# Attention with chunk selection and a wave mixer: batch 1's later keys copied once from PSUM, three blocks of u turned by DMA, and a new instruction order

## The chip, the cores and the metric

The kernel runs on one core of a Trainium2 chip. The metric is the device time of one launch in microseconds. A core has five engines that each run their own instruction stream in order: TensorE (PE in the profile, with its weight loads as PEld), VectorE (DVE), ScalarE (ACT), GpSimd (POOL) and SyncE (SP), which here issues all DMAs.

## The reference

The reference is selective attention followed by a mixer. Sizes: 4 batches, 8 heads, 768 positions, head size 64; the mixer's width is 512.

```python
k_chunks = k.reshape(B, H, nc, chunk, D)           # 24 chunks of 32 keys
k_min, k_max = k_chunks.min(axis=3), k_chunks.max(axis=3)
ub = sum(maximum(q * k_min, q * k_max), axis=-1)   # bound of each query for each chunk
top_chunks = argsort(where(causal, ub, -1e9))[..., -6:]
scores = where(selected & causal, q @ k.T / 8, -1e9)
x = softmax(scores) @ v                            # heads side by side: 4 x 768 x 512

theta = x @ w_theta
y = w_tok_r @ (x * cos(theta)) + w_tok_i @ (x * sin(theta))
u = x + y
out = u + maximum(u @ w_ch, 0)
```

## The kernel before, in words

The kernel records some 1,400 small operations in `record` and emits them in the order of the string `ORDER`. Each number there is an operation; a letter behind it picks another of the engines that the operation may run on ("b" the second, "c" the third of its list; no letter is the first). F with a number is a run of filler matmuls on PE. Every engine executes its share in the order of the string, so `ORDER` alone decides both who does what and when. Buffers are handed out by `decode` as the string is walked: each class in `CLASSES` has a fixed number of slots, and an operation that needs a slot waits for the last user of its former tenant. Loads have 6 slots ("ld"), PSUM has two wide score tiles ("sc"), one "av" bank and three general banks ("mi").

Attention works on pairs of heads, four pairs in a batch. For a pair of batches 1 to 3, `pair` (L417) loads keys and queries with 128 positions to a partition row, and turns them on PE with the help of an identity (L434), 384 positions to a PSUM bank. It does this:

- Keys. For each half of the positions, four instructions read the bank: two copies of one head each into the fp16 key tile `kx` (the `evk` operations), and a maximum and a minimum over each chunk (`red0`, `red1`, L451), which give the chunk bounds `km`.
- Queries. One fp32 copy per half into `qT` (`evq`), two fp16 casts from it into `qx` (`cq`), and a relu of it (`relu`, on DVE or POOL at L195, on ACT at L197).
- Bounds and selection. `group` (L474) multiplies bounds and queries of two pairs (`ub`, L491), turns the result on DVE, takes the sixth largest value of each query, and copies a mask into rows 64 to 88 of `qx` (`cp`, L536). `kx` has the matching one-hot rows, so a score product adds the penalty by itself.

`heads` (L543) forms scores in three steps per head (`sc`, L564), takes the exponential on ACT (`ex`, L570), zeroes the later triangle (`tri`, POOL at L580 or DVE at L578), and multiplies with v (`av`, L402); DVE divides by the sum (`norm`, L412 and L413). Batch 0 does the same with other tiles (`row_pair`, `row_heads`).

`mixer` (L587) then turns x (on PE for batches 0 and 1, by DMA from SP for 2 and 3, L600), multiplies by w_theta (`th`, L617), takes sin and cos on ACT (L624, L628), forms `z`, and for each of six blocks of 128 rows multiplies by the token weights (`mix`, L640 and L642: twelve matmuls of 512 columns). DVE adds x (`u`, L648). Each block of u is turned, and multiplied by w_ch (`ch`, L673); DVE forms the output (`ot`, L678) and SP stores it. How a block is turned hangs on a set:

```python
if (b, t) in U_DMA:
    op("SP", f"Du.{b}.{t}", 1270, [(u[t], 0)], [(uT[t], 0)], ...)   # one DMA transpose
    continue
ps = buf("mi", f"ups.{b}.{t}", (DM,), FP16)                         # else PE and a copy
op("PE", f"Tu.{b}.{t}", 220, [(u[t], 0)], [(ps, 0)], tr)
ev16(f"evu.{b}.{t}", ps, uT[t], DM)
```

The weights are loaded during batch 0, cast to fp16 by POOL, ACT or DVE, and turned by DMA (token weights of four row blocks) or by PE (of two). In the string, attention of batch b+1 is woven into the mixer of batch b.

The set `K_SB` is in the code already, and empty. A pair in it copies its turned keys to a tile `kT` and works from there:

```python
kT = buf("qT", f"kT.{b}.{p}") if (b, p) in K_SB else None
...
for x in range(2) if kT is not None else ():
    copies(f"ck.{b}.{p}.{x}", S, 0, False, [(kT, 0), (kT, 1)], [(kx, (x, 0)), (kx, (x, 1))], ...)
```

Of the kernel before, what the change touches and what calls it, by code (L numbers as in the profile page):

```python
# [15 lines left out]

ORDER = (
    "10|"
    "3 2 448 4 449b 404b 1 722b 475b 29 28 31 30 0 21 57 17 58 9 18 5 721 19b 14 7 15 56 6 F9 32 20c 10 36 55 "
    "11 35 39 48 12 F17 44 34 13b 8 41 33 85 23 45 75 16c 42 37 47b 38 22 24 84 40 25 F15 50 102 26 68 27 403 "  # L20
    "71 51 69 180 82 52 72 174 181 83 63 175 74 165 65 182 59 64 166 171 49 373 60 374 61 172 168 176b 53 115 "
    "169 67 54 F7 177 173 167b 77 62b 43 46b 170b 178 76c 95 78 125 66 206 179 191 79 96 189 207 103 188 192 "
    "200 80 183 113 208b 201 187 81 193 194 190 184 195 202 90 197 91 203 196 92 198 98 70c 86 73c 141 204 185 "
    "116 88 223 109 199 87 144 99 217 205 186 224 215 126 213 214 211 89 114 209 216 400 226 218 225 399 269 "
    "94 129 101 227 210 127 270 142 220 212 128b 104 133 110c 221 143 228b 219b 145 271 93 105 229 376 272b "
    "106 222 384 137 230 379 375 107 232 402 387 410 100 233 401 108 236 381 97 377 414 386 231 258 412b 380 "
    "234 255 146 385b 130 259 235 237 256 388 246 260 238 239 134 247 240 249 383 257 411b 241 111 250 252 153 "
    "248b 382 253 242 243 251 131 389b 474 378 413 244 273 254 263 132 267 138c 274b 135 245 262 159 266 136b "
    "265 139 268 261 390 140b 264 392 391 418 150 393 275 419 112 416 276 396b 405 394 123 277 417 408 117 "
    "422b 395 407b 162 281 409 278 154 406b 289 415b 147 160 425 155 290 420c 279 285 421c 282 161 280 283 426 "  # L30
    "124 286 435 156 297 427b 287 151 428 119 291 293 284 152 118b 315 288 299 316 429 121 298 317 292 397 295 "
    "301 430 163 302 294 436 437 318 148b 432c 446 308 434c 447 309 296 444 310 445 300 311 319 438 320 431 "
    "149 433 303 157 321 515 439 544 516 120c 304 158 122c 305 440c 347 306 443c 423 348 312 441c 307 468 313 "
    "545 517 471 528 314 343 442b 361 546 470 344b 529 557 164 362 461 463 558 462b 530 554 464b 455 398b 472 "
    "450 559 457b 560 363 465 322 451 459 473 323 452 458 324 467b 466c 494 325 453 456 326 561 454 327 424c "
    "741 345 555 534 328 460b 355 562 535 469 346 349 720 356 518 556 565 350 358 519 357 536b 481 719 359 520 "
    "476 483 563 479 547 482 717 336 477b 548 337 484 745 338 478 549 485 339 746 480 340 341 486b 718 487 342 "
    "489 488 531 495 490 364 743 532 492c 491 353 365 521 493b 541 789 533 522 564 496 742 566 354b 366 542 "
    "523 744 370 497 506 543 786 524 498 526 371 507b 734 736 787 508 329 737 330 735b 372 331 509 739b 332 "
    "499 738 788 333 740b 510 334 765 500 760 511c 335 525 761 360 728 512c 527 351 513c 730 758 352 586 729 "  # L40
    "514c 808 550 501 759 552 551 731 504c 367 587 732 764c 553 723 747 725 810 368 583 748 811 538 727 588 "
    "539 584 369 763 537 750 752 751 606 753 1053 502c 726 580 749 1054 585 755 607 733b 803 540 505c 503c 754 "
    "724b 609 608 804 756 619 762 581 621 620 790 757b 622b 766 591 793 570 792b 610 809 767 813 791b 812 582 "
    "571 794 1056 612 611 768 589 1055 590 613 777 572 573 795 592 769b 574 614 814 832 599 778b 796b 615 575 "
    "617 600 779 567 616 797 601 770 596 568 780 771 597 578 781 569 593 772 784c 576 785b 577 799 598 594 892 "
    "798 774c 618 819 800b 815 776c 898 1079 823 893 801 595 1080 579 775c 1078 899 895 894 816b 1077 802 603 "
    "900 818 885 896 807c 602 817 604 827 820b 623 886 605 882 828 879 897 624 883 903 887 625 822 805 902 880 "
    "626 1057 901 1061 884 631 821 806 904 627 633 1060 881 773 889 1058b 890 888 1059b 853 856 629 891 635 "
    "632 782 783 628 643 634 636 630 637 639 824 644 833c 647 645 638 1075 640 679 646 641 680 681 648 642 651 "
    "649 652 857 653 650 654 682 1076c 683 1120 684 1121 854 825 858 685 869 1099 655 826 855b 697 866 870 831 "  # L50
    "656 829 834 867 657 830 693 1068 835 872 868 1069 844 859 871 672 873 836 845b 837 673 1100b 874 674 846 "
    "658 860 1142 659 838 847 660 839 861 661 848 841b 699 840 851b 849 842 843b 662 852c 700 663 850c 877 701 "
    "875 664 908 918 694 909 1062 1086 1063b 876 919 910 947 1144 1090 675 1145 1089 1064 920 676 878 1087 677 "
    "1088 950 1065 864 862 1066 711 678 702 1067 712 696 1070 703 1094 1071 863 713 1095b 665 704 1073 948 865 "
    "1123 666 1081 1122 1072c 951 1092 1146 934 1084 949 1143b 1147 911 1093b 667 1166 1074 1082 668 1098b "
    "1096c 669 1085 1097 670 912 708 671 1083 1091b 935 924 952b 695 709 1101 925 913b 936b 1137 710 1102 926 "
    "905 1111 1103b 921 1138b 906 1112b 686 1104 1124 922 1135 907 1128 916 944 1105 1136 914 923b 931 1106 "
    "945 1139 915 1125b 705 1141b 917 1140 937 932 1127 687 1108c 706 927 1109c 929 1107b 688 1113 933 707 "
    "1110b 689 946 938 928 1114 1219 930 1167 1126 953 955 1213 1220 1115 939 1129 1214 954 1221 1132 1216 "
    "1117c 1133 941 1119c 1217 942 1131b 690 1215 691 956 1118c 1130 940 1218 1193 692 1226 1134b 1194 1116c "  # L60
    "1161 943 698 1148 1227 1195 1229 1162b 1222 1151 1223 1230 957 1228 1224 1149b 1232 1159 1225 1233 1153 "
    "1231 958 1206 1150 1157 1187 1234 1207 1160b 1236 1237 1156 959 1235 1188 1165c 714 1238 1154 1200 1152 "
    "961 1155 1190 715 1158b 1201 963 1189 1208 960 1191 1168 1163c 1164c 965 962 1202 1203 1169 1192 1198 "
    "1178 971 1170 1179b 716 1171 1196 964 1197 1180 967 972 973 1172 975 966 968 974 969 983 1199 976 979 977 "
    "970 985 1001 978 1002 981 1173 1003 980 1181 1004 1177 984 982 1022 1204 1023 986 1005 1182 994 1176 995 "
    "1184 996 1186 1183 1185b 1006 1174 1175b 1205 1255 1007 1258 1256 1209 1211 1031 1008 1009 1259 1257b "
    "1252 1260 1210 1253 1278 1212 997 1279 1010 1254b 1263 1239 1262 1280 1240 1261 1245 1264 998 1246 1024 "
    "1241b 1271 1025 1247 1272 1265 1026 1273b 1266 1242 1011 1243 1012 1267 1284 1027 1285 1244 1250 1281 "
    "1028 1286 1248 1249 1282 1034 1041 1251 1283 1268 1042 1013 1269 999 1043 1014 1288 1287 1270 1000 1276 "
    "1032 1289 1015 1290 1274 1275 1016 1030 1277 1017 1018 1019 1291 1020 1050 1021 1292 1044 1051 1293 1038 "  # L70
    "1045 987 1039 1294 1297 988 1299 1295 1301 989 1296 990 1298 991 1302 992 1300 1040 1305 1303 1033 993 "
    "1304b 1309 1306 1052 1307 1313 1046 1310 1029 1317 1311 1308 1314 1342 1312 1315 1343 1344 1319 1316 1345 "
    "1318 1335 1320 1336 1337 1338 1339 1340 1346 1341 1347 1328 1365 1348 1329 1330 1331 1366 1321 1322 1323 "
    "1324 1325 1326 1047 1327 1332 1048 1363 1333 1356 1334 1357 1049 1358 1359 1377 1380 1378 1364 1360 1381 "
    "1361 1379 1349 1382 1362 1350 1035 1351 1036 1352 1374 1037 1353 1375 1354 1369 1376 1355 1371 1370b 1367 "
    "1372 1389 1368b 1373 1386 1390 1383 1387 1391 1384 1388 1385 "
)

B, H, S, D = 4, 8, 768, 64
P = 128  # L80
DM = H * D
NT = S // P
CH = 32
NCH = S // CH
QS = 192
NS = S - QS
RUN = NS // 2
NB = RUN // CH
SCALE = float(1.0 / np.sqrt(D))
NEG = -1000.0  # L90
KX = D + NCH
ROW = (0,)
X_DMA = (2, 3)
K_SB = set()
LAST = (3, 4)
W_DMA = (2, 3, 4, 5)
U_DMA = {(b, t) for b in (1, 2, 3) for t in range(NT) if b < 3 or t < 4}
SEGS = [(0, 4), (1, 3), (2, 5)]
BASE = [0, 1024, 2048]

# [58 lines left out]
def record(G):  # L159
# [257 lines left out]
    def pair(b, p):  # L417
# [18 lines left out]

        kT = buf("qT", f"kT.{b}.{p}") if (b, p) in K_SB else None
        for f in range(2):
# [481 lines left out]
```

The softmax here doesn't subtract the row's maximum and nothing guards it: scores larger than these inputs give would overflow.

## Time and profile before

| | us |
|---|---|
| median of 4 runs (lowest to highest) | 227.96 (227.54 to 229.69) |
| the profiled execution, its own time | 227.6 |
| its span, first to last instruction | 225.9 |
| PE busy | 215.9 (96%) |
| DVE busy | 173.5 (77%) |
| ACT busy | 164.9 (73%) |
| POOL busy | 93.3 (41%) |
| 16 DMA engines, the hardware queue's share | 70.0% |

A row of a group gives the line, engine, operation, names and shapes, then the total busy time, the mean of one in ns, and the idle time of the engine just before these instructions with what ended it. Rows of stages give each engine's busy time in a stretch of the span, counted in us from its start. The granted PE clock is 1.00 all through.

### The profile page before, as it was taken

Reading aid. Unit: us, or ns where it says so; the run is one execution under the profiler, and the core shown is the slowest. Engines: PE = TensorE matmul, PEld = TensorE weight load, DVE = VectorE, ACT = ScalarE, POOL = GpSimd, SP = SyncE. Lnnn points to the kernel's source line nnn. Section 1 sums busy time; section 2 is a strip of 40 time slices with the busy share of each in tenths; the row PEclk is TensorE's granted clock in tenths of the full one; section 3 lists DMA queues with packets and bytes.
Section 4 is the critical chain, followed back from the end, with each engine's and each line's share of the span. In section 5 each row is a group of like instructions: output and inputs, shape, how many; then the busy total and the mean of one; then the engine's idle time right before and its main releaser. Section 6 shows DMA issues by size and latency. Waiting matters only on the chain.

```text
span 225.9 us, 5663 instructions
## 1 busy us (share of the span) xinstructions
PE 215.9 (96%) x2122; PEld 127.2 (56%) x2122; DVE 173.5 (77%) x505; ACT 164.9 (73%) x247; POOL 93.3 (41%) x190
## 2 busy tenths in 40 slices
PE   7999999989999999888999999999989999999993
PEld 2765766834566667566545665677445564444441
DVE  4699789699889699899977899999885366242553
ACT  2759999999498758999998559899998870560011
POOL 8524647554424648869306223586401130300000
PEclk9999999999999999999999999999999999999999
DMA  6999899999999999976038469413511025562254
GB/s 162 272 263 233 274 312 279 244 304 208 288 251 211 280 254 279 235 179 139 4 70 186 120 115 262 115 48 68 101 47 23 3 70 101 88 186 46 79 178 164
DMA packets 103471, 38.07 MB, mean 169 GB/s; under 512 B 97436, under 2 KB 97820, under 8 KB 103444
## 3 DMA queue, kind: packets, MB, share of 16 engines
q1 hardware_dynamic: 103444, 37.71, 70.0%
q8 instruction: 17, 0.28, 0.5%
q14 instruction: 10, 0.08, 0.1%
HBM read 26.17 MB, written 6.29 MB: 144 GB/s over the span
## 4 chain that ended last, share of the span: by engine, by line
PE 73%; ACT 13%; DVE 4%; DMA 3%; SPq 3%; issue 1%; DVEq 0%; ACTq 0%
PE y L640 13%; PE y L642 13%; PE sc L564 9%; PE ch L673 8%; PE av L402 7%; PE th L617 6%; ACT pt L358 4%; ACT pt L570 3%; PE qps L434 2%; PE kps L434 2%; PE ub L491 2%; PE ub L278 2%; SPq L600 2%; ACT kx L169 2%; DMA xT<-x 2%; PE sc L342 2%
## 5 line engine op out<-in xcount | busy, mean ns | idle before, releaser
L570 ACT ACTIVATE pt<-sc 128x1024 f16<-128x1024 f32 (+1 forms) x72 | 63.3, 919 | 8.8 <-PE sc L564 8.1
L640 PE MATMUL y<-z,wtokT 128*128 128x512 f16 x144 | 54.6, 379 | 0.1
L642 PE MATMUL y<-z,wtokT 128*128 128x512 f16 x144 | 54.5, 379 | 0.0
L580 POOL TENSOR_SCALAR_AFFINE_SELECT pt<-pt 128x256 f16<-128x256 f16 x62 | 25.5, 416 | 49.1 <-ACT pt L570 47.7
L564 PE MATMUL sc<-qx,kx 88*128 88x512 f16 (+3 forms) x192 | 37.2, 305 | 1.2 <-ACT pt L570 1.0
L402 PE MATMUL av<-v,pt 128*128 128x65 f16 x672 | 30.6, 194 | 0.9 <-ACT pt L570 0.8
L402 PEld LDWEIGHTS <-pt 128*128 128x128 f16 x672 | 27.6, 98 | 6.9 <-ACT pt L570 1.4
L648 DVE TENSOR_TENSOR u<-y,x 128x512 f16<-128x512 f32 x24 | 16.4, 689 | 14.3 <-PE y L642 14.1
L451 DVE TENSOR_REDUCE km<-kps 128x12 f32<-128x384 f32 x48 | 25.1, 545 | 1.5 <-PE kps L434 1.1
L617 PE MATMUL th<-wtheta,xT 128*128 128x512 f16 x96 | 22.7, 379 | 1.6 <-DVE ubT L507 0.9
L564 PEld LDWEIGHTS <-kx 88*128 88x128 f16 x192 | 16.6, 97 | 13.2 <-issue 2.6
L673 PE MATMUL ch<-wch,uT 128*128 128x512 f16 (+1 forms) x96 | 23.6, 374 | 0.0
L642 PEld LDWEIGHTS <-wtokT 128*128 128x128 f16 x144 | 14.0, 98 | 15.1 <-issue 0.9
L640 PEld LDWEIGHTS <-wtokT 128*128 128x128 f16 x144 | 14.0, 97 | 15.1
L678 DVE SCALAR_TENSOR_TENSOR ot<-ch,u 128x512 f32<-128x512 f32 (+1 forms) x24 | 16.3, 678 | 7.5 <-PE ch L673 7.3
L632 DVE TENSOR_TENSOR z<-x,cs 128x1024 f16<-128x1024 f16 x23 | 17.0, 759 | 5.8 <-ACT cs L628 3.5
L628 ACT ACTIVATE cs<-th,pi 128x512 f16<-128x512 f32 x24 | 16.2, 697 | 6.8 <-PE th L617 6.3
L169 ACT COPY qT<-qps 128x384 f32<-128x384 f32 x24 | 11.2, 485 | 13.6 <-PE qps L434 6.9
L358 ACT ACTIVATE pt<-sc 128x1024 f16<-128x1024 f32 (+1 forms) x24 | 20.9, 928 | 0.3 <-PE sc L350 0.2
L172 POOL CAST qx<-qT 64x768 f16<-64x768 f32 (+1 forms) x18 | 14.5, 812 | 10.6 <-ACT qT L169 6.5
L413 DVE TENSOR_TENSOR x<-av,rec 128x384 f16<-128x384 f32 x32 | 17.8, 557 | 1.1
L169 ACT CAST kx<-kps 64x384 f16<-64x384 f32 (+1 forms) x36 | 16.8, 478 | 2.3 <-PE kps L434 1.0
(103 smaller groups left out, 339.0 us busy)
## 6 DMA issues: line engine op xcount, KB each, us to landing
q<-in_q_dram SPq DMA_DIRECT2D x32, 192.0 KB, 3.7
k<-in_k_dram SPq DMA_DIRECT2D x32, 192.0 KB, 3.7
v<-in_v_dram SPq DMA_DIRECT2D x16, 384.0 KB, 4.1
out_dram<-ot SPq DMA_DIRECT2D x23, 256.0 KB, 2.3
wtok<-in_moe_w_tok_r_dram SPq DMA_DIRECT2D x6, 384.0 KB, 4.4
wtok<-in_moe_w_tok_i_dram SPq DMA_DIRECT2D x6, 384.0 KB, 5.5
wth<-in_moe_w_theta_dram SPq DMA_DIRECT2D x4, 256.0 KB, 4.2
wch<-in_moe_w_ch_dram SPq DMA_DIRECT2D x4, 256.0 KB, 5.5
```

The source lines that it names most:

```text
L169: c = {"A": ("ACT", int(n * 0.833 + 60), 0, lambda: nc.scalar.copy(out=out(), in_=in_())), "D": ("DVE", int(n / 0.96 + 70) if psum else in ...
L358: nc.scalar.activation(out=T(pt)[:, :, base:base + w], in_=T(ps).rearrange("p (x c) -> p x c", x=2)[:, :, 0:w], func=AF.Exp, bias=0.0, sca ...
L402: nc.tensor.matmul(ps[:, t, :], T(pt)[:, x, o:o + P], T(v16)[:, x, j, :], start=(j == 0), stop=(j == t))
L413: nc.vector.tensor_tensor(out=T(x16)[:, :, h * D:(h + 1) * D], in0=ps[:, :, 0:D], in1=T(rec).broadcast_to([P, NT, D]), op=ALU.mult)
L451: nc.vector.tensor_reduce(out=T(km)[:, j, 12 * f:12 * f + 12], in_=src.rearrange("p (c w) -> p c w", w=CH), axis=AX.X, op=o)
L564: nc.tensor.matmul(T(ps)[:, a0:a1], T(kx)[0:KX, x, j * P:(j + 1) * P], T(qx)[0:KX, x, q0 + a0 - o:q0 + a1 - o], start=True, stop=True)
L570: nc.scalar.activation(out=T(pt)[:, x, BASE[s]:BASE[s] + w], in_=T(ps)[:, 0:w], func=AF.Exp, bias=0.0, scale=SCALE)
L580: eng.affine_select(out=a, in_=a, pattern=[[0, 2], [1, P]], compare_op=ALU.is_ge, fill=G.zero_reg(), base=0, channel_multiplier=-1)
L617: nc.tensor.matmul(T(ps), T(xT[t])[:, c, :] if by_dma else T(xT[c])[:, t * P:(t + 1) * P], K.wtheta[:, c, :], start=(c == 0), stop=(c == 3))
L640: nc.tensor.matmul(T(ps), K.wtok[:, si, 0, t * P:(t + 1) * P], T(z[si])[:, 0], start=(si == 0), stop=False)
L642: nc.tensor.matmul(T(ps), K.wtok[:, si, 1, t * P:(t + 1) * P], T(z[si])[:, 1], start=False, stop=(si == NT - 1))
L673: nc.tensor.matmul(T(ps)[:, 0:n1 - n0], T(uT[t])[:, c * P:(c + 1) * P], K.wch[:, c, n0:n1], start=(c == 0), stop=(c == 3))
```

## The change

Three constants change; no line of a function does.

- `K_SB` holds pairs 2 and 3 of batch 1. Their turned keys leave each PSUM bank in one fp32 copy of 128 x 384 to `kT` (a slot of the class "qT"); the chunk maxima and minima read `kT`, and two casts of 64 x 768 per pair make the fp16 keys.
- `U_DMA` holds blocks 3, 4 and 5 of batch 0 too. Each is turned by one DMA transpose from SP in place of four matmuls and a copy out of PSUM.
- `ORDER` is another string. Apart from the operations above, 112 operations run on another engine than before, and nearly all stand in another place. There are 43 filler matmuls in it where there were 48.

```diff
-    "3 2 448 4 449b 404b 1 722b 475b 29 28 31 30 0 21 57 17 58 9 18 5 721 19b 14 7 15 56 6 F9 32 20c 10 36 55 "
...
+    "2 3 0 1 401b 29 28 4 30 31 400 21 58 5 57 9 12 56 F7 32 8 36 55 6 719 14 35 7 472 17 39 48 11 446 15 18 "
...
-K_SB = set()
+K_SB = {(1, 2), (1, 3)}
 LAST = (3, 4)
 W_DMA = (2, 3, 4, 5)
-U_DMA = {(b, t) for b in (1, 2, 3) for t in range(NT) if b < 3 or t < 4}
+U_DMA = {(b, t) for b in range(4) for t in range(NT) if (b < 3 or t < 4) and (b, t) not in ((0, 0), (0, 1), (0, 2))}
```

Counted over the two strings, the moves between engines are these (operations before, then after):

| | ACT | DVE | POOL |
|---|---|---|---|
| key copies out of PSUM (`evk`) | 36, 32 | 20, 20 | - |
| key casts (`ck`) | 0, 2 | 0, 1 | 0, 1 |
| query copies (`evq`) | 24, 23 | 8, 9 | - |
| query casts (`cq`) | 3, 5 | 11, 9 | 18, 18 |
| relus | 8, 6 | 4, 3 | 4, 7 |
| mask copies (`cp`) | 9, 14 | 14, 9 | 25, 25 |
| triangles (`tri`) | - | 17, 6 | 79, 90 |
| weight casts | 2, 7 | 4, 4 | 14, 9 |
| v casts (`cv`) | 3, 5 | 4, 3 | 9, 8 |
| turned u (`evu`) | 4, 2 | 4, 3 | - |

The order of SP's loads and of its DMA transposes changes with the string as well: at the start the keys of the first pair come first, and the three new transposes stand among the loads of batch 2.

## Prediction

> **What bounds the kernel now.** I read the page's first two parts first, then single matmuls in the timeline, then busy times by stage, then the chain of waits inside the one stage that stood out, and last the groups with their shapes kept apart.
>
> ```profile
> PE 215.9 (96%) x2122; PEld 127.2 (56%) x2122; DVE 173.5 (77%) x505; ACT 164.9 (73%) x247; POOL 93.3 (41%) x190
> ...
> PEclk9999999999999999999999999999999999999999
> DMA  6999899999999999976038469413511025562254
> ```
>
> TensorE (PE) looks full, at full clock throughout, and the DMA engines are full until slice 17 (about 96 us). But the next view shows how little "busy" means for PE.
>
> ```profile
> 150.88 0.38 PE L640 MATMUL y<-z,wtokT 128*128 128x512 f16 x1
> 151.10 0.38 PE L642 MATMUL y<-z,wtokT 128*128 128x512 f16 x1
> 151.31 0.38 PE L640 MATMUL y<-z,wtokT 128*128 128x512 f16 x1
> ```
>
> Each row lasts 0.38 us, yet the next starts 0.22 us later. The page's 96% would leave 10 us of PE outside its work. The Trainium skill (Perfetto Trace Analysis, "Identifying the Most-Contended Engine") calls matmul busy share a poor measure because matmuls overlap; so I count the distance between starts, taken where nothing waits: mixing pair 0.43, head's score step 0.43/0.43/0.27, block of th or ch 0.86, three turns 0.33, one ub 1.13 (1.33 in batch 0). Over all of PE's instructions that gives 205 us. The span is 225.9, so some 21 us are start, end and stalls, and a new order can move those. Where they sit, by stage (us of each engine in each stretch):
>
> ```profile
> 46.00:54.00 8.00, 7.05 (x58) 2.73 (x56) 7.72 (x21) 7.45 (x13) 3.70 (x7) 1.00 1.13 222
> 54.00:86.00 32.00, 32.00 (x273) 19.23 (x272) 27.38 (x82) 23.47 (x37) 15.17 (x30) 1.00 1.14 266
> 86.00:104.00 18.00, 15.62 (x214) 10.78 (x211) 16.96 (x56) 16.89 (x26) 14.20 (x32) 1.00 0.87 206
> 104.00:120.00 16.00, 16.00 (x148) 9.56 (x145) 13.66 (x30) 15.91 (x25) 5.52 (x9) 1.00 0.34 77
> ```
>
> The columns are length, PE, weight loads, DVE, ACT, POOL, clock, DMA share, GB/s. From 54 to 86 PE never rests, while ACT is idle for 8.5 us. From 86 to 104 ACT and DVE are nearly full and PE loses 2.4 us of busy time. The chain of waits there runs through ACT:
>
> ```profile
> 87.57 0.48 ACT kx L169
> ...
> 88.54 0.92 ACT pt L570
> ...
> 97.39 0.70 ACT pt L570
> ...
> 98.62 1.94 ACT pt L570 x2
> ```
>
> These are key evictions of batch 2 and exponentials of batch 1. So two regimes follow each other: PE-bound, then ACT-bound. From 104 us the PE stalls are small.
>
> **The change, part by part.** Prices come from these rows:
>
> ```profile
> L169 ACT CAST kx<-kps 64x384 f16<-64x384 f32 x29 | 13.6, 473 | 1.6 <-PE kps L434 1.0 <-DVE km L451 0.2
> L171 DVE CAST kx<-kps 64x384 f16<-64x384 f32 x19 | 10.4, 547 | 1.1 <-PE kps L434 0.9
> L195 POOL TENSOR_SCALAR qr<-qT 128x576 f32<-128x576 f32 x4 | 6.6, 1646 | 1.9 <-ACT qT L169 1.2 <-DVE qT L171 0.6
> L593 ACT COPY uT<-ups 128x512 f16<-128x512 f16 x4 | 2.3, 587 | 19.9 <-PE ups L661 19.9
> ```
>
> and, of the turned u (issue times of SP, then issue to landing):
>
> ```profile
> L654 SPq DMA_TRANSPOSE uT<-u x16: 1189/1200/2047, 119.7 to 213.1; - x16
> ...
> DMA to landing us min/median/max: 2.4/2.5/4.0
> ```
>
> *Keys of two pairs.* Eight half-width copies out of PSUM go (six of 0.47 on ACT, two of 0.55 on DVE: 3.9 us); four full-width copies come, three on ACT (0.485 by the row of qT) and one on DVE (0.55), 2.0 us; four casts from SBUF come, two on ACT (0.83), one on DVE (0.56 by the median of that cast of queries), one on POOL (0.87), 3.1 us. Sum: +1.2 us, spread over three engines. In return a PSUM bank has one reader instead of four, about 1.5 us less hold for each of four banks. The group of key turns has 0.0 us of idle before it, so I value it at nothing; if the bank is the bound, it gains up to 1.5 us once. The reductions (0.545 from PSUM) now read SBUF, which no row shows; I take the same price, with 0.4 and 0.6 as ends, 8 x 0.1 on DVE. A rule speaks against the casts: the Trainium skill (SBUF — State Buffer, "Who interferes with whom") says a DVE copy or cast that runs in its two-port mode locks POOL out for its whole length, while a reduction doesn't. The row for the same cast of queries on DVE has median 0.56 and longest 1.17 us. By the rule POOL loses the whole 0.5 to 1.2 us once; by the row the DVE cast costs 0.56 and POOL has 5 us of idle time in each 10 there. I take nothing, and 1.2 us as the upper end.
>
> *Turned u of three blocks.* PE loses 3 turns of 4 x 0.055: -0.66 us. One eviction leaves ACT (0.59), two leave DVE (0.41 each). Three DMAs of 1.2 us issue join SP's queue, +3.6 us. They stand behind Lv.1.3, Lk.2.1.1 and Lq.2.2.1, and the loads of batch 2 stand behind them. Before, those loads land 2 to 7 us ahead of their turns; I take 0, with 1.5 as upper end. Then the wait: between the last mixing product of the block and its ch the new order has 9.8 us of PE work for block 3, 9.9 for block 5, 6.9 for block 4. The way round is 0.9 (u on DVE with latency), 0.5 of SP, and 2.5 to 4.0 landing; with DMA full I take 4.0: 5.4 us. All three are covered, block 4 by 1.5 us; if DVE or SP is more than that late, ch of block 4 and all PE behind it wait.
>
> *New order.* It moves most. Over the whole program, with the distances between starts, ACT goes from 144.3 to 149.9 us, DVE from 158.8 to 154.9, POOL from 80.6 to 84.5; the sin/exp table changes stay 8. DVE sheds 11 triangle masks and 5 nsT copies; ACT takes weight copies and five nsT copies; POOL takes the masks and goes from 4 to 7 relus at 1.65 us (ACT 0.69, DVE 0.45).
>
> Until batch 0's mixing the two orders cost the same. From the first exponential to the first sin/cos ACT has 30.3 us in both, and the first mixing product waits for the same cos of block 3 (33.9 then, 33.4 now). At the start the ninth load gates the last q turn in both. One new wait: DVE casts wch.3 ahead of the first z; it was 4.9 us from issue to use before, on POOL. Behind it queue cq, z and the two ub transposes that free PSUM for th of blocks 5 and 4. I put +0.4 against the -0.4 of the mixing's start.
>
> The stage that decides is first mixing product to last exponential of batch 1, before 53.84 to 101.04 = 47.2 us. Sums inside it:
> - PE 44.0 before, so stalls are 3.2; now 42.5 (three turns less; the rest of the difference is work ordered to other places).
> - ACT 34.1 before with one table load, traced 37.6 busy (ratio 1.10); now 39.0, so 43.0. It has 3 more weight copies, 1 more of v, 2 cq, 2 qT, 2 nsT and the 2 key casts (7.1 us); 3 key copies, a relu and a turned-u eviction fewer (2.2 us).
> - DVE 38.7 before, traced 41.9 (1.08); now 35.3, so 38.2.
>
> So the exponentials are spread: by the end of block 5's mixing ACT has 20.1 us of work where it had 14.2, beside 21.3 of PE where it had 20.5. The ACT idle time of 54 to 86 gets used, but by added work as much as by old work. Now every helper must be read against PE: before, PE 44.0 with the fullest helper (DVE) at 41.9 lost 3.2; now PE 42.5 has ACT at 43.0. I let the stall grow by the same 1.1 us: 4.3. Bounds: ACT needs 43.0 - 42.5 = 0.5 at least; if ACT keeps 6.5 of the 9.6 us (47.2 - 37.6) idle, 7.0.
>
> After that: PE and ACT work up to the end are equal within 0.5 us, and DVE has 2.8 us less queued ahead of th of batch 2 (PE 1.0 less), where th of block 3 waited 0.9 us for its turned x. But th of block 0 now needs the second turned x instead of the first (+1.26 of SP). I take -0.3 (+1 to -0.9). Out and end are alike.
>
> Sum against the profiled execution (227.6; span 225.9 and 1.7 around it): -0.66 + 1.1 - 0.3 = +0.1, so 227.7. The median of the runs shown is 0.36 higher, so **228.0**.
>
> **The rivals.**
> - *The interleaving pays.* PE, ACT and DVE are full in different places before and evenly after; DVE's 3.7 us less in the stage speaks for it, as does ACT's idle 8.5 us. Stall 1.0 instead of 3.2: -0.66 - 2.2, so 225.1. Against it: from 86 to 104 nearly full helpers already cost PE 2.4 us busy time.
> - *ACT becomes the bound of the stage (slower).* In-order ACT gets 4.9 us more here, among it casts of weights that wait on DMA and of queries. Place: exponentials of batch 1 between the mixing of blocks 0 and 4. It decides from the point where ACT stays idle more than 3.4 us in the stage; at 6.5 us the stall is 7.0, +3.8 - 0.66, so 231.1. For it: ACT idled 5 us from 75 to 101 too, with its exponentials late. Against it: those waits were for PE's scores, which now come earlier.
> - *The turned u comes late.* 1.5 us at ch of block 4, or loads behind it: 228.0 + 1.5 = 229.5.
> - *The change doesn't do what it says:* the three turns and eight copies are gone from the instruction streams, so only the timing is open.
>
> **How the numbers follow.** About 1% (2.3 us) is what a measurement of this kernel can tell from no change. Forecast 0.44 (its own range 226.3 to 229.7), interleaving 0.24, ACT bound 0.26, late u 0.06. Faster by over 1% (under 225.7) is most of the second case and the forecast's lower edge: 0.23; slower (over 230.2) is most of the third, with parts of the fourth and first: 0.30; the rest 0.47. The range reaches from the interleaving case to a little over the ACT case, 224.9 to 231.4.
>
> **What would show it.** PE's rows of turned u fall from 32 to 20, uT DMAs rise from 16 to 19; evenly busy ACT from 54 to 104 (over 22 of 24 us in each half) shows the spreading. PE stalls there of 1 or of 7 us show a rival; waits on uT before ch show the late turn. I am wrong if the stalls come before 54 us or after 104 us, where I kept the old ones: a cast waiting on its weight's DMA in DVE's or ACT's queue would do it, or POOL's relus holding a mask that av needs.

## The result and the profile after

The changed kernel takes 226.68 us (median of 32 runs, 225.70 to 229.55) where the kernel before, run beside it, takes 228.22 (median of 51). The ratio is 0.993, with a 95% interval from 0.9914 to 0.9947. It is faster by 1.5 us, or 0.7%. The forecast was no change (228.0); the time lies in its range, and in the middle one of its three cases (225.7 to 230.2), but a small gain is there that it did not see. The profiled execution took 226.34 us with a span of 224.6.

The lines of the page that answer to those of before, first the busy times and the slices, then the groups of what was removed and added:

```profile
PE 216.5 (96%) x2105; PEld 127.3 (57%) x2105; DVE 166.5 (74%) x484; ACT 170.9 (76%) x254; POOL 98.1 (44%) x201
...
DMA  7999989999999999989159469316600164662434
```

```profile
L195 POOL TENSOR_SCALAR qr<-qT 128x576 f32<-128x576 f32 x7 | 11.5, 1644 | 3.3 <-ACT qT L169 1.7 <-DVE qT L171 1.5
L169 ACT CAST kx<-kps 64x384 f16<-64x384 f32 x23 | 10.9, 472 | 0.9 <-PE kps L434 0.6
L451 DVE TENSOR_REDUCE km<-kT 128x12 f32<-128x384 f32 x8 | 4.0, 547 | 0.2 <-ACT kT L169 0.2
L169 ACT CAST kx<-kT 64x768 f16<-64x768 f32 x2 | 1.7, 831 | 0.0
L169 ACT COPY kT<-kps 128x384 f32<-128x384 f32 x3 | 1.3, 467 | 0.0
```

The prices of the forecast hold: 0.47 for a full-width copy, 0.83 for a cast on ACT, and 0.547 for a reduction from SBUF, the same as from PSUM. The work went where it was expected. The stages say where time was won (length, then PE, weight loads, DVE, ACT, POOL, clock, DMA share, GB/s):

```profile
46.00:54.00 8.00, 6.75 (x58) 3.19 (x57) 7.96 (x24) 7.58 (x13) 1.11 (x2) 1.00 1.10 262
54.00:86.00 32.00, 32.00 (x271) 19.08 (x268) 25.39 (x80) 29.82 (x47) 14.02 (x27) 1.00 1.09 233
86.00:104.00 18.00, 17.08 (x229) 11.91 (x228) 17.22 (x57) 17.51 (x28) 14.34 (x30) 1.00 1.05 256
```

From 54 to 86 us PE stays full while ACT goes from 23.47 to 29.82 us: 6.4 us more on ACT, and PE does not feel it. From 86 to 104 PE is busy for 17.08 us instead of 15.62, and ACT for 17.51 instead of 16.89. The groups of that stretch of 18 us show what changed hands, first of the kernel before (PE alone), then of the changed one:

```profile
L564 PE MATMUL sc<-qx,kx 88*128 88x512 f16 (+3 forms) x38 | 7.6, 306 | 1.2 <-ACT pt L570 1.0
L402 PE MATMUL av<-v,pt 128*128 128x65 f16 x101 | 4.7, 194 | 0.9 <-ACT pt L570 0.8
```

```profile
L570 ACT ACTIVATE pt<-sc 128x1024 f16<-128x1024 f32 (+1 forms) x16 | 13.8, 914 | 0.3 <-PE sc L564 0.3
...
L564 PE MATMUL sc<-qx,kx 88*128 88x512 f16 (+3 forms) x39 | 7.8, 304 | 0.6 <-ACT pt L570 0.5
L402 PE MATMUL av<-v,pt 128*128 128x65 f16 x105 | 4.8, 194 | 0.0
...
L673 PE MATMUL ch<-wch,uT 128*128 128x512 f16 x8 | 2.0, 377 | 0.1
```

ACT has 16 exponentials there; before it was 14 (12.3 us). PE waits 0.6 us at scores and 0.0 at the products with v, where it waited 1.2 and 0.9. Two blocks of ch (8 matmuls) stand in the stretch instead of one. The last exponential of batch 1 starts at 99.19 us, 44.46 after the first mixing product (54.73); before, it was 47.20. With the 42.5 us of PE work counted for that stage, its stall is 2.0 us. The forecast said 4.3, and before it was 3.2.

The stage has two parts, which meet where the 13th exponential of batch 1 starts (86.44 us before, 85.84 after). Two rows of the kernel before, then two of the changed kernel:

```profile
53.84:86.44 32.60, 32.60 (x280) 19.64 (x280) 27.98 (x83) 23.85 (x37) 15.52 (x31) 1.00 1.14 265
86.44:101.04 14.60, 12.87 (x183) 8.92 (x181) 13.91 (x48) 13.71 (x21) 11.48 (x25) 1.00 0.98 234
```

```profile
54.73:85.84 31.11, 31.11 (x266) 18.73 (x265) 24.50 (x76) 28.93 (x45) 13.86 (x27) 1.00 1.10 234
85.84:99.19 13.35, 12.67 (x165) 8.46 (x164) 12.80 (x45) 12.90 (x21) 10.29 (x22) 1.00 1.03 254
```

In the first part PE never rests, before or after. The 13th exponential is the first to write into a buffer from which products with v still read, and in all 18 traces of this case it starts 0.1 us behind the last of these products. It comes 1.5 us earlier because PE has less to do ahead of them: three turns of u, a mixing pair and a block of ch fewer, one key turn more, 1.6 us by the forecast's prices. In the second part ACT hardly rests. It got 1.3 us shorter because ACT has one mask copy (0.43 us) less there and is idle for 0.45 us instead of 0.89.

The chain of waits does not tell the two kernels apart by kind. It runs through exponentials and passes to PE in the middle of the stretch in both, from 93.36 to 97.39 us before (first fence) and from 91.81 to 96.41 after:

```profile
93.36 0.36 PE av L402 x6
...
96.42 0.66 PE kps L434 x6
```

```profile
89.43 1.47 ACT pt L570 x2
...
91.81 1.02 PE ch L673 x4
...
94.33 1.13 PE ub L491 x32
...
96.41 1.62 ACT pt L570 x2
```

### The profile page after: what moved, and what is told of

Same layout as the page of the kernel before. It is cut to its first block, busy times and chain, and to the rows that moved or that the text cites. A ratio compares the mean times of both kernels' runs of the same rounds, so it can differ in the third digit from the quotient of the medians.

```text
span 224.6 us, 5637 instructions
## 1 busy us (share of the span) xinstructions
PE 216.5 (96%) x2105; PEld 127.3 (57%) x2105; DVE 166.5 (74%) x484; ACT 170.9 (76%) x254; POOL 98.1 (44%) x201
## 4 chain that ended last, share of the span: by engine, by line
PE 72%; ACT 15%; DVE 7%; DMA 1%; issue 1%; SPq 1%; ACTq 0%
PE y L640 14%; PE y L642 14%; ACT pt L570 9%; PE ch L673 8%; PE sc L564 8%; PE th L617 6%; PE av L402 5%; ACT kx L169 2%; PE qps L434 2%; PE ub L491 2%; PE ub L278 2%; PE warm L844 2%; PE sc L342 2%; DVE km L451 2%; PE kps L434 2%; DMA xT<-x 1%
## 5 line engine op out<-in xcount | busy, mean ns | idle before, releaser
L642 PE MATMUL y<-z,wtokT 128*128 128x512 f16 x144 | 54.5, 379 | 0.0
L580 POOL TENSOR_SCALAR_AFFINE_SELECT pt<-pt 128x256 f16<-128x256 f16 x69 | 27.9, 409 | 27.9 <-ACT pt L570 26.7
L564 PE MATMUL sc<-qx,kx 88*128 88x512 f16 (+3 forms) x192 | 38.1, 306 | 0.8 <-ACT pt L570 0.5
L402 PEld LDWEIGHTS <-pt 128*128 128x128 f16 x672 | 27.1, 98 | 8.2 <-issue 1.9
L673 PE MATMUL ch<-wch,uT 128*128 128x512 f16 (+1 forms) x96 | 23.9, 374 | 0.1
L451 DVE TENSOR_REDUCE km<-kps 128x12 f32<-128x384 f32 x40 | 20.5, 546 | 1.0 <-PE kps L434 0.8
L632 DVE TENSOR_TENSOR z<-x,cs 128x1024 f16<-128x1024 f16 x24 | 15.9, 680 | 4.7 <-ACT cs L624 3.7
L169 ACT CAST kx<-kps 64x384 f16<-64x384 f32 (+1 forms) x29 | 13.6, 476 | 6.1 <-PE kps L231 5.2
L536 POOL COPY qx<-nsT 24x288 f16<-24x288 f16 x25 | 10.8, 436 | 11.7 <-DVE nsT L528 10.8
```

The source lines that it names most:

```text
L169: c = {"A": ("ACT", int(n * 0.833 + 60), 0, lambda: nc.scalar.copy(out=out(), in_=in_())), "D": ("DVE", int(n / 0.96 + 70) if psum else in ...
L402: nc.tensor.matmul(ps[:, t, :], T(pt)[:, x, o:o + P], T(v16)[:, x, j, :], start=(j == 0), stop=(j == t))
L451: nc.vector.tensor_reduce(out=T(km)[:, j, 12 * f:12 * f + 12], in_=src.rearrange("p (c w) -> p c w", w=CH), axis=AX.X, op=o)
L564: nc.tensor.matmul(T(ps)[:, a0:a1], T(kx)[0:KX, x, j * P:(j + 1) * P], T(qx)[0:KX, x, q0 + a0 - o:q0 + a1 - o], start=True, stop=True)
L580: eng.affine_select(out=a, in_=a, pattern=[[0, 2], [1, P]], compare_op=ALU.is_ge, fill=G.zero_reg(), base=0, channel_multiplier=-1)
L642: nc.tensor.matmul(T(ps), K.wtok[:, si, 1, t * P:(t + 1) * P], T(z[si])[:, 1], start=False, stop=(si == NT - 1))
```

## The experiments

The kernels below were made from the two orders; a diff shows moved operations by name and engine. Their line numbers are smaller by 3 than those of the page (L567 is the exponential, L431 the turn, L448 the reduction). Ratios are to the kernel before.

**Each part taken out of the changed kernel.** First the turned u.

```diff
-U_DMA = {... and (b, t) not in ((0, 0), (0, 1), (0, 2))}      # u.0.3, Du.0.3 (SP)
+U_DMA = {(b, t) for b in (1, 2, 3) ...}                       # u.0.3, Tu.0.3 (PE), evu.0.3 (DVE)
```

> The changed kernel, but blocks 3, 4 and 5 of u are turned by PE and copied out of PSUM again (each turn about 0.1 us behind its u, the copies on DVE, ACT and DVE as before). The new order and the copied keys stay. Theory A (the gain comes from the new order, which spreads the exponentials of batch 1 over the mixing of batch 0; the DMA turns are worth only their PE time): 226.7 + 0.7 = 227.4, ratio to before 0.996. Theory B (the gain comes from the turned u that PE and PSUM no longer handle; the order is neutral): 228.2 or above, ratio 1.000.

Measured: 228.35 us, ratio 0.9997 (0.9972 to 1.0023). Against 0.993 the DMA turns are worth 0.67%, 1.5 us. PE's own time explains 0.66 of it. A part of the rest stands in PE's timeline, as a wait that the changed kernel does not have:

```profile
70.65 0.55 PE L431 MATMUL kps<-ident,k 128*128 128x128 f32 x3 [0.23 <-DVE ot L675]
```

A turn on PE needs one of the three general PSUM banks, and here a key turn waits for a bank that an output still reads. In this order a bank is worth something too. From 90 to 110 us PE's stalls are as in the changed kernel (2.9 us against 2.8), so what was won there does not come from the DMA turns.

Then the keys.

```diff
-K_SB = {(1, 2), (1, 3)}      # evk.1.2.0 (ACT) ... red1, red0 up to 40 places on, ck.1.2.x
+K_SB = set()                 # evk.1.2.0.0 (ACT), evk.1.2.0.1 (ACT), red0, red1
```

> The changed kernel, but the keys of pairs 2 and 3 of batch 1 are read four times from PSUM as before (the two half-width copies stand where the one copy stood, the two reductions right behind them); the new order and the DMA turns stay. Theory A (order): 226.7 within 0.4, ratio 0.993. Theory B, in the form that the shorter hold of the PSUM banks gives the gain: 1.0 to 1.5 us longer, 227.7 to 228.2, ratio 0.998 to 1.000.

Measured: 229.70 us, ratio 1.0067 (1.0041 to 1.0093), 1.4% or 3.1 us above the changed kernel, twice what theory B gave. The executions are of two kinds. Nine have a mean granted clock of 0.998 or more and a median of 228.81; 13 have one of 0.989 to 0.993 and a median of 230.81. So about 2 us of the 3.1 are there at the full clock, and about 1 comes with the lower one. PE's timeline of the profiled execution (clock 0.999) from 66 to 86 us, where the changed kernel shows no wait at all, has these:

```profile
72.13 0.52 PE L431 MATMUL kps<-ident,k 128*128 128x128 f32 x3 [1.02 <-ACT pt L567]
73.67 0.39 PE L637 MATMUL y<-z,wtokT 128*128 128x512 f16 x1 [1.02 <-DVE km L448]
74.94 1.02 PE L670 MATMUL ch<-wch,uT 128*128 128x512 f16 x4 [0.24 <-DVE km L448]
```

DVE's timeline of the same run shows why:

```profile
70.96 1.02 DVE L448 TENSOR_REDUCE km<-kps 128x12 f32<-128x384 f32 x2 [0.69 <-ACT kx L166]
```

The reductions begin when ACT's two half-width copies of that bank (from 69.98) are done: the row names a semaphore of ACT as what they waited for. So the bank is held for two copies and then 1.02 us of reductions; the turn at 72.13, whose bank this is, follows their end at 71.98 (the row puts its wait down to an exponential that ended at the same moment). The forecast's hold of 1.5 us more for each bank was right. Its value was not: the new order puts the four key turns between 69.3 and 71.4 us, where the order before had 6 us of mixing between the first two (64.5) and the last two (71.1).

**Which part of the keys' readers counts.** Two runs, of which the first is the control for the second.

```diff
-evk.1.2.0 (ACT), ..., red1.1.2.0, ..., red0.1.2.0
+evk.1.2.0 (ACT), red0.1.2.0, red1.1.2.0            # all four banks; reads kT as before
```

> The changed kernel with the eight reductions of keys of pairs 2 and 3 of batch 1 moved right behind the copy that they follow (they read the copy in SBUF, as in the changed kernel). It is the control for the next run: it moves 4.4 us of DVE work forward by up to 4 us and leaves the PSUM banks as they are. If only the hold of the banks matters: 226.7, ratio 0.993, within 0.5. If the place of DVE's work is what the run with keys from PSUM lost by: 228 to 229.7, ratio 1.000 to 1.007.

```diff
-src = T(ps)[:, 0:384] if kT is None else T(kT)[:, fs]
+src = T(ps)[:, 0:384]
```

> As the run with the reductions drawn forward, except that they read the keys in PSUM and not the copy, so each bank is held until the copy and both reductions are done. The half-width copies stay away: ACT and DVE have the same work as in that run. Theory H (the bank's hold is what the single copy takes away): PE waits 1.5 to 3 us at the key turns and the products behind them, so 1.5 to 3 us above that run, 228.2 to 229.7. Theory J (the gain is ACT's and DVE's shorter work, or the half-width copies' place in their queues): as that run, within 0.4.

Measured: the control 227.51 us, ratio 0.9962 (0.9941 to 0.9982); with the reductions on PSUM 227.61, ratio 0.9961 (0.9942 to 0.9981). PE's waits from 66 to 86 us, of the control and of the other:

```profile
72.75 1.02 PE L670 MATMUL ch<-wch,uT 128*128 128x512 f16 x4 [0.62 <-DVE kT L168]
```

```profile
71.15 0.52 PE L431 MATMUL kps<-ident,k 128*128 128x128 f32 x3 [0.53 <-DVE km L448]
71.99 0.39 PE L637 MATMUL y<-z,wtokT 128*128 128x512 f16 x1 [0.32 <-DVE km L448]
73.38 1.04 PE L670 MATMUL ch<-wch,uT 128*128 128x512 f16 x4 [0.35 <-DVE km L448]
```

The waits for reductions are there (1.2 us in sum against 0.6), but the medians differ by 0.1 us, with intervals of half a microsecond. Theory H is not confirmed at the size it claimed; the times are those of theory J. So the 3.1 us split, as an estimate from the ratios, into about 0.7 for DVE's reductions being drawn forward (they can't stay behind when they hold a bank), 0 to 0.6 for reductions that hold a bank, about 1.0 for the lower clock, and 0.8 to 1.4 for what remains, the half-width copies. These keep a bank 0.5 us longer as well, and were not tried alone.

**The parts without the order, and the order without the parts.**

```diff
 (old order)
-u.0.3, Tu.0.3 (PE), evu.0.3 (DVE); evk.1.2.0.0, evk.1.2.0.1, red0, red1
+u.0.3, Du.0.3 (SP);                evk.1.2.0, red0, red1, ck.1.2.0, ck.1.2.1
```

> The order and the engines of the kernel before, with both parts put into it: blocks 3, 4 and 5 of u turned by DMA right behind their u, keys of the two pairs copied once. Theory A (order): the parts bring 0.66 us of PE at most, and in the old order ch of blocks 4 and 5 follows the mixing after 2.5 to 4.4 us of PE work, less than the 5.4 us of the way round through DMA, so 227.6 to 229.5, ratio 0.997 to 1.006. Theory B (parts): the gain of the change is already here, 226.7, ratio 0.993.

Measured: 235.84 us, ratio 1.0323 (1.0285 to 1.0361), far beyond both theories. PE's timeline:

```profile
83.51 1.89 PE L670 MATMUL ch<-wch,uT 128*128 128x512 f16 x4 [3.78 <-DMA uT<-u]
92.99 1.04 PE L670 MATMUL ch<-wch,uT 128*128 128x512 f16 x4 [1.15 <-DMA uT<-u]
```

The turn by DMA came 3.8 us late for block 5 and 1.2 late for block 4. In the old order, ch follows too soon. More is lost behind the first wait: these four matmuls of ch took 1.89 us where four take 1.04 at the second wait, because the granted clock was 0.50 for 3.4 us from 82.86 on (the eighth number of the row):

```profile
82.90:86.20 3.30, 2.69 (x18) 1.60 (x19) 0.77 (x3) 0.00 (x0) 0.00 (x0) 0.50 1.13 286
```

All six executions of this run have a mean granted clock between 0.985 and 0.993.

```diff
 (old order)
-evk.1.2.0.0 (ACT), evk.1.2.0.1 (ACT), red0, red1
+evk.1.2.0 (ACT), red0, red1, ck.1.2.0 (POOL), ck.1.2.1 (DVE)
```

> The order and the engines of the kernel before, with only the keys of pairs 2 and 3 of batch 1 copied once (casts on the engines of the changed kernel); blocks 3 to 5 of u stay on PE. Theory A' (the single copy is worth much only because the new order puts all four key turns within 2 us of one another; in the old order, where they are 10 us apart, the banks have time): as before, 228.2 within 0.6, ratio 0.997 to 1.003. Theory B' (the single copy is a gain in itself): 1.5 to 3 us faster, 225.2 to 226.7, ratio 0.987 to 0.993.

Measured: 229.80 us, ratio 1.0078 (1.0041 to 1.0115). Neither theory: the single copy alone makes the old order slower, by 1.9 us. One new wait is in PE's timeline, a turn of u that waits 0.96 us for u on DVE; that DVE's and ACT's order was not fitted to the new casts is my reading, and no run tests it.

```diff
 (new order)
-K_SB = {(1, 2), (1, 3)}; Du.0.3, Du.0.4, Du.0.5
+K_SB = set(); Tu.0.3, Tu.0.4, Tu.0.5 with their copies
```

> The new order alone: blocks 3 to 5 of u on PE, keys read four times from PSUM. If the parts' worth in the new order adds up (1.7 for u and 3.0 for the keys by the two runs that took one of them away): 226.7 + 4.7 = 231.4, ratio to before 1.014: the new order alone is slower than the old. If one stall covers the other (both wait for the same three PSUM banks): 229.7 to 230.4, ratio 1.007 to 1.010.

Measured: 231.52 us, ratio 1.0161 (1.0105 to 1.0217). The new order alone is slower than the old by 1.6%. The time is that of parts whose worths add up, but this is not shown: the interval is 1.3 us to either side, and the clock has a share in it here too. Four of the six executions have a mean granted clock of 0.992 or 0.993. The profiled one is among them; its clock was 0.50 from 73.37 us on, amid waits of about 1 us for the key banks:

```profile
73.40:76.70 3.30, 2.89 (x10) 1.59 (x11) 2.76 (x7) 1.15 (x3) 0.00 (x0) 0.50 1.06 257
```

So neither order nor parts hold the gain: every mixture of old and new is as slow as before or slower.

**What was won from 86 to 104 us.** From the run with u on PE, the ch of two blocks is put back to where the old order had it.

```diff
-Tu.0.5, evu.0.5, ... 15 PE operations ..., ch.0.5, ch.0.4
+Tu.0.5, evu.0.5, ... 4 ..., ch.0.5, ...; Tu.0.4, evu.0.4, ... 4 ..., ch.0.4
```

> As the run of the new order with u on PE, and the ch of blocks 5 and 4 (with their outputs) drawn forward from 87 and 92 us to three and four PE instructions behind the turn of their u, as in the kernel before. Theory F (the new order gains from 90 to 110 us because ch of two blocks is held back as PE work for the stretch that waits for exponentials): stalls there rise from 2.9 by 1.0 to 1.5 us, so 229.3 to 229.9. Theory G (it gains there because exponentials of batch 1 are done earlier): 228.35 as that run, within 0.4.

Measured: 229.97 us, ratio 1.0098 (1.0061 to 1.0135), 1.0% above the run it came from (0.9997), which is theory F's size. PE's waits from 86 to 104 us, where that run has 0.6 in this row:

```profile
PE sc L561 <- ACT pt L567: 1.9, 4, 0.8
```

But these waits are not where the time went. From the 13th exponential of batch 1 to the last it is 13.2 us here and 13.35 in the run it came from. What grew is the part ahead of it, from the first mixing product to the 13th exponential: 35.3 us instead of 32.5. Both blocks of ch (0.86 us each) now stand in front of the products with v for which this exponential waits: they end at 89.02 and it starts at 89.12, though its score was done at 87.49. The two blocks are 1.7 of the 2.8 us, and 0.7 are two waits of this trace near 57 us. So ch held back is worth the earlier exponentials (theory G's cause), and not the waits that it fills.

The converse: the old order with only this taken over.

```diff
 (old order)
-ch.0.5 at 79 us, ch.0.4 at 86 us
+..., Tq.2.2.1, ch.0.5, sc.1.7.1, Tx.1.0, Tx.1.1, ch.0.4, Tk.2.2.0, ...
```

> The kernel before (old order, neither part) with one thing of the new order: ch of blocks 5 and 4 of batch 0 (with their outputs) held back, from 79 and 86 us to 91 and 93 us, where PE waits for exponentials (stalls of 0.72 and 0.27 us stand just there, 4.35 in all from 90 to 110). Theory F (held-back ch fills those waits): 0.7 to 1.4 us faster than before, ratio 0.994 to 0.997. Theory G (only earlier exponentials help): ratio 1.000 within 0.002; if ch takes banks that the turns of batch 2 need, 1.002 to 1.006.

Measured: 229.47 us, ratio 1.0053 (1.0026 to 1.0081). Slower: theory F, in the simple form that work held back fills the waits, falls. ACT's waits from 86 to 104 us in this run:

```profile
ACT pt L567 <- PE sc L561: 1.4, 2, 1.2
ACT xT L590 <- PE xps L605: 0.6, 1, 0.6
ACT pt L567 <- PE av L399: 0.5, 1, 0.5
```

PE no longer waited at the score where ch stood, but the scores behind ch came late, and ACT, which bounds the stretch, idled 2.5 us there (0.8 before, 0.3 in the changed kernel). The 13th exponential came earlier here too (32.0 us behind the first mixing product instead of 32.6), but from it to the last it is 16.4 us instead of 14.6. Held-back work pays only where PE has finished in time what ACT needs next. Why the new order leaves room for it and the old does not was not tried further.

```diff
-ch.0.3 at 78 us
+..., sc.1.7.2, ch.0.3, sc.1.6.2, ch.0.4, ...
```

> The changed kernel with ch of block 3 too held back, from 78 us to 91 us, in front of the score product that waits 0.64 us there for an exponential. Theory F: 0.5 us faster than the changed kernel, 226.2, ratio 0.991. If the banks or DVE's outputs there are already full: 226.7 to 227.5, ratio 0.993 to 0.996.

Measured: 227.11 us, ratio 0.9956 (0.9932 to 0.9981). No gain from a third block; the wait of 0.47 us in front of the score became one of 0.82 in front of ch, and the part from the 13th exponential to the last takes 14.6 us instead of 13.35.

**Whether ACT's sum decides.** The step of the forecast that grew the stall rests on ACT's work from the first mixing product to the last exponential of batch 1. Three runs change that sum: less of it early, more of it late, more of it early.

```diff
-cwch.2, cwtok.1.3, cwtok.0.4, cwtok.1.4, cq.1.3.1, cv.2.0 (ACT)      122b 151b 154b 157b 489b 739b
+the same (POOL)                                                      122  151  154  157  489  739
```

> The changed kernel with six casts between 54 and 81 us put from ACT onto POOL (three of token weights, one of a channel weight, one of queries, one of v): 4.8 us less on ACT in that stretch, at nearly the same price on POOL, which is busy there for 14 of 32 us. Theory P (my forecast's step: ACT's total from the first mixing product to the last exponential of batch 1 sets the stall): 1.3 to 2.4 us faster than the changed kernel, 224.3 to 225.4, ratio 0.983 to 0.987. Theory Q (PE bounds that stretch and ACT's work there is hidden): 226.7 within 0.4, ratio 0.993.

```diff
-cq.2.0.0, cq.2.0.1 (POOL)
+cq.2.0.0, cq.2.0.1 (ACT)
```

> The changed kernel with two casts of queries of batch 2 (91.7 and 93.0 us, 0.83 each) put from POOL onto ACT, between exponentials of batch 1. Theory Q (ACT's exponentials bound the stretch from 86 to 104): 1.2 to 1.7 us slower than the changed kernel, 227.9 to 228.4, ratio 0.998 to 1.001. If ACT has slack there too: 226.7 within 0.4.

```diff
-cv.1.0, cv.1.2 (POOL)
+cv.1.0, cv.1.2 (ACT)
```

> The changed kernel with two casts of v (60.1 and 73.2 us, 0.83 each) put from POOL onto ACT: the same amount as in the run that loads ACT from 91 to 94, but earlier. Theory P: the same loss as in that run, 1.2 to 1.7 us. Theory Q: 226.7 within 0.4, ratio 0.993.

Measured: relieved 226.95 us, ratio 0.9918 (0.9888 to 0.9949); loaded late 228.82, ratio 0.9995 (0.9972 to 1.0019); loaded early 228.21, ratio 0.9962 (0.9943 to 0.9982). The stages of the relieved run:

```profile
54.00:86.00 32.00, 32.00 (x250) 18.51 (x249) 25.64 (x86) 25.46 (x40) 17.43 (x31) 1.00 1.13 244
86.00:104.00 18.00, 17.03 (x232) 11.71 (x231) 17.06 (x56) 17.11 (x27) 13.94 (x30) 1.00 1.02 238
```

ACT has 4.4 us less from 54 to 86, PE is full either way, and the time is that of the changed kernel. DVE's busy time stayed the same there (25.64 us, 25.39 in the changed kernel), so POOL's added casts did not eat up a gain by holding DVE up. Theory P asked for a ratio of 0.987 at most, which the interval excludes. Loading ACT late costs 0.65% or 1.5 us for 1.66 us of work, as theory Q said; PE's waits from 86 to 104 us:

```profile
PE sc L561 <- ACT pt L567: 1.0, 3, 0.5
PE sc L561 <- POOL pt L577: 0.4, 1, 0.4
```

Loading it early was neither as dear as theory P had it nor free as in theory Q: 0.3% or 0.7 us. The timeline names a place:

```profile
62.81 0.61 PE L561 MATMUL sc<-qx,kx 88*128 88x512 f16 x3 [0.59 <-ACT qx L533]
```

A score waits for a mask copy that stands behind the added cast. So PE feels single operations that it needs next, not a sum: ACT's work can be taken away for nothing where PE does not wait for it, and costs in front of something awaited (0.7 of 1.66 us early, 1.5 of 1.66 late).

The stage's two parts, in one trace of each run, say the same (us; "first part" is from the first mixing product of batch 0 to the 13th exponential of batch 1, "second part" from there to the start of the last):

| | first part | second part |
|---|---|---|
| before | 32.6 | 14.6 |
| changed | 31.1 | 13.35 |
| new order, u on PE | 32.5 | 13.35 |
| new order, keys from PSUM | 34.9 | 13.35 |
| new order, neither part | 36.5 | 13.35 |
| old order, both parts | 38.4 | 15.9 |
| ACT relieved early | 31.4 | 13.7 |
| ACT loaded late | 31.15 | 14.8 |
| ACT loaded early | 32.8 | 13.35 |

The second part belongs to the order: in the new one its 13.35 us return whatever is done to the parts, and 1.4 of the 1.66 us of ACT loaded late are added to it. What the DMA turns and the copied keys save, they save in the first part.

**The start.** Two runs concern the wait before th of block 5: 1.25 us of idle PE in the changed kernel's trace, 0.87 before (the expectations count it as 1.42).

```diff
-old order up to mix.0.0.0, then old order
+old order up to mix.0.0.0, then new order (both parts in)
```

> The order before up to the first mixing product of batch 0, the new order from there, both parts in. Theory A (order): the new order loses about 0.4 us of PE ahead of the mixing (a stall of 1.42 us before th of block 5, where DVE casts a channel weight ahead of the first z) and gains behind it; so 226.2, ratio 0.991, faster than the changed kernel. Theory B (parts) or if the gain came ahead of the mixing: 226.7 or more, ratio 0.993 or above.

Measured: 228.15 us, ratio 0.9999 (0.9973 to 1.0026). This run tells little: where the two orders meet, from 56 to 65 us, PE waits 2.0 us in three places that neither kernel has.

```diff
-cwch.3 (DVE)
+cwch.3 (POOL)
```

> The changed kernel with one cast, of the last channel weight, back on POOL as before (0.62 us there, 1.06 on DVE), so that DVE comes 1 us sooner to the first z and to the two ub copies that th of blocks 5 and 4 wait for. If that wait (1.42 us before th of block 5) decides the start of the mixing: 0.5 to 1.0 us faster than the changed kernel, 225.7 to 226.2, ratio 0.989 to 0.991. If the z of the last blocks decide it in any case: 226.7 within 0.3.

Measured: 226.37 us, ratio 0.9933 (0.9910 to 0.9957): nothing won. The rows of DVE and POOL tell where the 1.06 us of the cast went:

```profile
46.51 0.87 DVE L168 CAST qx<-qT 64x768 f16<-64x768 f32 x1
48.81 0.80 DVE L201 TENSOR_TENSOR km<-km 128x24 f32<-128x24 f32 x1
```

```profile
46.28 0.69 POOL L169 CAST wch<-wch 128x512 f16<-128x512 f32 x1
48.70 0.88 POOL L169 CAST wtok<-wtok 128x768 f16<-128x768 f32 x1 [1.73 <-PE th L614]
```

In the changed kernel the same two DVE instructions take 0.56 and 0.17 us. Here each starts while a POOL cast runs and ends just behind it, which gives back 0.94 us.

Last, the relief and this cast together:

```diff
-cwch.3 (DVE); cwch.2, cwtok.1.3, cwtok.0.4, cwtok.1.4, cq.1.3.1, cv.2.0 (ACT)
+all seven on POOL
```

> The run that relieves ACT from 54 to 80, with the cast of the last channel weight on POOL as well. Theory P: 224.0 to 225.4. Theory Q: 226.4 within 0.4, as the cast on POOL alone, ratio 0.992.

Measured: 227.66 us, ratio 0.9937 (0.9917 to 0.9958): theory Q by the ratio. No run beats the changed kernel beyond its interval.

## Why the prediction was wrong, step by step

- *Stall of the deciding stage, +1.1 us: this is the step that failed.* The stall was read as PE against the fullest helper, and "I let the stall grow by the same 1.1 us: 4.3". It fell from 3.2 to 2.0. ACT's sum itself was nearly right (41.8 us busy in the stage, forecast 43.0); what failed is holding it against PE over the whole stage. The stage has two parts. In the first PE is full, and 4.4 us of ACT's work can go without any effect (the relieved run); in the second ACT's work counts nearly in full (1.5 us for 1.66). ACT's added time went to the first part (28.9 us busy instead of 23.9), and in the second ACT has less than before (12.9 instead of 13.7). So ACT became fuller where it does not bound, and the stall shrank where it does. I had counted ACT's 20.1 us "by the end of block 5's mixing" and seen ACT's idle 8.5 us, and then put the whole sum against PE all the same.
- *Keys valued at nothing: wrong in this order.* The price of the copies and the 1.5 us less hold were right, but 0.0 us of idle at the key turns of before says nothing of an order that puts the turns close together. There the copy is worth about 2 us at the full clock and 3.1 in the median.
- *Errors that cancel.* That the middle of the forecast is only 1.3 us off is in part luck. It took the parts for -0.66 and the order for +1.1 - 0.3. By the runs the parts are worth about -1.5 and -3.1 in the new order, and the order alone costs +3.6.
- *Turned u, -0.66: a size too small.* Measured 1.5 us in the new order. The cushions held, though less than was thought: u of block 4 was ready at 84.11 us, SP issued its transpose at 87.3, and ch began at 91.81, 4.5 us behind; with this trace's landings (median 2.8, longest 4.5) that left, by estimate, 0 to 1.7 us. SP ran 3 to 4 us behind for all three blocks, where I had allowed 0.5. The late-u rival was real: in the old order it costs 3.8 and 1.2 us.
- *Start, +0.4 against -0.4: not refuted.* In one pair of traces the first mixing product comes 0.89 us later (54.73 against 53.84), but over all traces it starts at 54.3 us on average with the old order ahead of it (5 traces) and at 54.5 with the new (13). That is a difference of 0.2 amid a spread of 2 us. The new wait was there; taking away the cast that was held for its cause won nothing.
- *th of batch 2, -0.3: right.* The wait for its turned x is 0.28 us, where it was 0.75. From the last exponential of batch 1 to the end it is 125.4 us instead of 124.9, which fits the 0.8 us of PE work that the forecast had moved behind the stage.
- *The rivals.* By the stall "the interleaving pays" was nearest (it said 1.0, the forecast 4.3, measured 2.0); by the time it was not (225.1, against 228.0 and a measured 226.68). ACT did become fuller, and idles only 2.7 us from 54 to 104, yet the slower outcome did not follow, for the reason of the first point. The signs named for it were right: turned u on PE in 5 blocks instead of 8, 19 transposes, and ACT busy 29.8 of 32 and 17.5 of 18 us.

## What to carry to other kernels

When a stage changes its bound halfway, a helper's work must be summed for each part and held against who is waited for there; one sum over both told the wrong sign here. Work held back pays by what it lets pass, so look for what stands behind it in the queue, and not for waits that it could fill. The value of an edit that frees a buffer or moves work to a slow queue belongs to the order around it: the same order and edits were worth -1.5 us together, and 0 to +7.4 us in every mixture with the old ones (at the upper end with the granted clock halved for a while), so neither an edit nor an order can be priced from the trace of a kernel that is arranged otherwise.

## What the runs showed of the hardware

- *DVE and POOL wait for each other.* An SBUF-to-SBUF instruction of DVE that starts while POOL works (mostly on a cast) is often stretched until that work is done: over the 18 traces of this case this befell 15 of 16 triangle masks of batches 1 to 3, 8 of 13 small differences of chunk bounds (`km`) and 12 of 26 z. Its end then lies a fixed time behind the end of the cast (0.41 us for a cast of queries, 0.54 for most of the stretched z, 0.15 for most of the masks). Of 140 additions that read PSUM and began beside a POOL instruction none was stretched by half. The other direction is there as well: all 18 POOL casts of 64 x 768 queries that began inside a DVE cast of queries took 1.13 to 1.22 us instead of 0.82, and all 13 mask copies on POOL that began inside a z of DVE 0.82 instead of 0.42. The forecast quoted the Trainium skill (SBUF — State Buffer, "Who interferes with whom") for one direction alone, DVE holding POOL up; the same section says that whichever starts first keeps the other out, and these rows agree. It explains the row of 1.17 us that the forecast read as the cast's own length: that cast began 0.16 us behind a POOL cast. Moving work off DVE onto POOL can thus give nothing.
- *The clock fell where PE waited.* In two traces the granted clock was 0.50 for 3.4 us amid waits of PE, from 82.86 us (a wait of 3.78 us, old order with both parts) and from 73.37 us (waits of 0.93 and 1.04 us, new order with neither part). In the trace of the new order with keys from PSUM it stayed at 1.00 through two waits of 1.02 us, but 13 of that run's 22 executions have a lower mean clock and are 2.0 us longer by the median. From which wait on the clock falls was not measured. A long wait can thus cost more than its length.
- *A bank's readers took turns.* In no pair out of 1419 did an instruction of ACT and one of DVE that read the same PSUM tile overlap, over the 18 traces, although both only read. The reductions of a key bank waited for a semaphore of ACT's copies (0.69 us of idle before them), so it is the program that keeps them apart; what the bank would allow, no run shows.
- *The start varies.* The first mixing product starts anywhere from 53.6 to 55.7 us over all traces, and from 53.6 to 55.3 in those of one and the same order up to there, more than the whole gain; two profiles must be compared from a common operation on, not by their spans. What varies was not settled.
